# A fused attention and expert kernel: values of batches 0 and 1 in one transfer, 129-column rows, empty slots left out of the gathers, and a new order of steps

## The chip, the cores and the metric

The kernel runs on one core of a Trainium2 chip. The metric is the device time of one execution in microseconds. Three executions of the kernel before took 221.56, 222.04 and 222.4 us; the median is 222.04 us. A core has five engines with instruction streams of their own that meet only at semaphores: PE multiplies matrices, DVE and ACT work on tiles element by element, POOL issues nearly all DMA transfers here, and SP issues the first few. Each engine takes its instructions strictly in the order of its own stream.

## The reference

Attention without a softmax over pairs: queries are normalised over the head dimension, keys over the sequence, and per batch and head a 64x64 matrix is built from keys and values. The rows that come out are sorted by a hash of a token id to one of 8 experts, each two matrix products with a ReLU between.

```python
def _attn_ref(q, k, v):            # 8 batches, 8 heads, 576 rows, 64 columns
    q_s = np.exp(q - max);  q_s = q_s / (sum over columns + 1e-09)
    k_s = np.exp(k - max);  k_s = k_s / (sum over rows + 1e-09)
    kv = np.einsum('bhsd,bhse->bhde', k_s, v)
    return np.einsum('bhsd,bhde->bhse', q_s, kv)
def _moe_ref(x, token_ids, w1, w2):   # x: 4608 x 512, 8 experts, 512 -> 1024 -> 512
    expert_idx = token_ids * 2654435761 % 8
    for e in range(8):
        mask = expert_idx == e
        out[mask] = np.maximum(x[mask] @ w1[e], 0.0) @ w2[e]
```

## The kernel before

Each expert has 640 slots: 72 for each of the 8 batches, and 64 for rows beyond 72 of a batch (overflow). The prologue (`_Index.core`) finds on DVE and PE, from the token ids, which row of q belongs to which slot and leaves the row numbers in `gidx`; `row` holds the numbers of the output rows, with a number beyond the last row where a slot is empty. A gather (L396) fetches 128 rows of q for 128 slots by an indirect DMA, and a row number out of bounds is left out of it. In the kernel before only overflow gathers and the scatters of the results (L550) have such numbers; an empty slot of a main gather fetches some valid row.

After the prologue all work is cut into named steps, and the text `ORDER` is the order in which they are issued, on every engine at once: an engine's own stream is what is left of `ORDER` when the steps of other engines are struck out. `SWAP` names steps that go to the other one of DVE and ACT than is usual. `NAME*n` puts n idle matmuls of 512 columns (L346) into the step's PSUM bank ahead of it. The steps that the prediction speaks of:

- `G e_i`: gather of block i of expert e (`GO_i`: of overflow); `EQ`: its exponential on ACT (L406); `SM`: sums over columns and reciprocals on DVE (L416 to L418) for two or three blocks; `ML`: the scaling on DVE (L422); `TP`, `TC`: transposes on PE (L432) and their copy (L895).
- `K b`, `V b`: transfer of keys and values of batch b, values cast to f16. Batches 0 to 2 of the keys go through SP's queue, and values of 0 and 1 through POOL's, all issued before the ordered part. `EK b`: exponential of keys on ACT (L355, L356); `MK b`: ones in the last column of the values on ACT (L361), so that the product also gives the column sums; `KV b`: 20 matmuls of 129 columns (L373) into a bank of the PSUM tag "S"; `SC b`: reciprocal and scaling on DVE (L382 to L388) into `kvr`.
- `CNT`, `OVA`, `OHA`, `FND`, `FDD`, `QS`, `ROP`, `ROD`: the places of overflow rows, on DVE but for FND and ROP (PE). `ZO0`, `ZO1`: zeros for the overflow gathers, on DVE. `XP`, `XC`, `SH`, `SD`, `SI`, `SE`: the overflow rows' products (PE) and their evacuation.
- `ANY`: a register load of a flag and a branch on every engine (L835, L836) around a general path that is not taken with these ids. That path uses the PSUM banks of tag "S" on PE, DVE and ACT. At the end of the branch each engine sets a mark when all its earlier steps are done.
- `PP`, `PC`: products of queries with `kvr` (L443) and their evacuation into `XT` (L925), the input of the experts.
- `W e1_i`, `W e2_i`: fetches of an expert's weights, in halves or whole (`WHOLE`). Two buffers each, so a fetch for expert e waits for the last use by expert e-2; keys of batches borrow the buffers of expert 1 before.
- `A e_lo_i`: first layer (L523) with `R`, its ReLU; `B e_blk`: second layer (L545) with `C`, its evacuation; `S e_blk`: scatter.

DMA transfers of POOL's queue run one after the other; SP's queue runs beside it on the same 16 DMA engines.

Of the kernel before, what the change touches and what calls it, by code (L numbers as in the profile page):

```python
# [695 lines left out]
PC0_00 MLOb TP1_3 MK6 TC1_2 PP1_02 KV4 TC1_3 SD2 G3_1 PP1_03 PC1_02 TPO_3 EK7 SC5 MK7 SH0 SC4 TCO_3 G2_1 PC1_03 KV6
G2_2 TPO_2 SC6 TCO_2 PP0_41 SD3 KV7 SD0 PC0_41 PP0_43 PP0_42 SC7 XP2 PC0_42 PP0_40 PC0_43 PC0_40 PP1_01 XP3 PC1_01
PP0_61 XC2 G3_0 PP0_62 G3_2 PC0_61 PP1_43 XC3 PC0_62 W11_1 PP1_40 PC1_43 SI1 PC1_40 SI3 PP1_42 PP1_00 SE1 G3_3 PC1_42
PC1_00 A0_0_2 SI0 EQ3_1 SE3 PP0_63 A0_0_0 W11_0 PP0_60 G2_3 R0_0_2 SE0 W02_1 SI2 PC0_63 PP1_41 EQ3_0 R0_0_0 W02_0 G5_2
EQ2_1 G4_4 SM3a A0_0_1 R0_0_1 PC0_60 SE2 A0_0_3 PC1_41 ML3a R0_0_3 A0_576_0 EQ2_2 A0_432_0 A0_432_1 TP3_1 OV1 EQ2_0  # L700
R0_432_0 A1_0_0 R0_432_1 A1_320_3 G2_4 SM2a TP3_0 R1_0_0 ML2a TC3_1 EQ3_3 TC3_0 A1_0_3 TP2_1 R1_320_3 R1_0_3 TC2_1
W12_0 EQ3_2 A1_0_2 SM3b TP2_2 TC2_2 R0_576_0 TP2_0 A1_320_2 W12_1 EQ2_3 G6_2 G4_1 R1_320_2 ML3b B0_0 G5_3 TC2_0 B0_4
EQ2_4 C0_0 PP2_02 SM2b PC2_02 TP3_2 ML2b B0_1 TP3_3 A1_320_1 TC3_2 W21_0 G4_2 OV2 TP2_3 TC3_3 R1_0_2 TC2_3 TP2_4
A1_320_0 C0_4 C0_1 G7_2 G5_0 PP2_32 W21_1 R1_320_0 PC2_32 G4_3 TC2_4 B0_2 PP2_31 C0_2 PP2_03 PC2_31 PC2_03 A1_0_1
PP2_01 R1_0_1 B0_3 EQ5_3 S0_2 PP2_00 W31_0 OV4 PC2_00 R1_320_1 PC2_01 C0_3 B1_0 G5_1 PP2_33 G4_0 EQ5_2 EQ5_0 G7_3
# [10 lines left out]
R5_320_1 S1_0 TC6_4 R5_320_0 S2_2 OV6 W52_1 S1_3 A4_0_0 R4_0_0 TP6_0 S3_2 TP7_0 W52_0 C3_4 W61_0 A5_0_1 PP6_60 PC6_60
B4_1 A5_320_2 B4_4 TC7_0 C4_1 TC6_0 R5_0_1 S4_1 R5_320_2 C4_4 A5_0_0 R5_0_0 PP6_01 B4_0 C4_0 A5_0_2 R5_0_2 B4_3 PP6_00
PC6_01 PP6_31 PC6_00 PC6_31 B5_1 C4_3 S3_1 S3_4 C5_1 PP6_30 PP6_61 B4_2 PC6_30 C4_2 PC6_61 A6_0_2 A6_0_1 R6_0_1 B5_2
A6_320_1 R6_0_2 B5_3 W71_0 A6_0_0 S4_3 C5_3 B5_4 W62_0 OV7 R6_320_1 C5_4 A6_0_3 R6_0_0 R6_0_3 A6_320_0 C5_2 S4_2 B5_0
A7_0_2 S5_1 R6_320_0 A6_320_3 B6_0 R7_0_2 R6_320_3 S5_3 A6_320_2 S4_4 A7_320_0 C6_0 R6_320_2 S5_2 A7_320_2 R7_320_2  # L720
# [64 lines left out]

# [240 lines left out]
```

## Time and profile before

| | before |
|---|---|
| median of 3 runs | 222.04 us |
| profiled execution, its own time | 222.7 us |
| span of the profiled execution | 220.9 us |
| PE busy | 187.5 us (85%), 1534 matmuls |
| DVE busy | 133.6 us (60%) |
| ACT busy | 113.7 us (51%) |
| POOL busy | 120.2 us (54%) |
| DMA moved | 50.67 MB, 229 GB/s on average |

How to read it: the span runs from the first to the last instruction, and the execution's own time is 1.8 us longer, for what lies around it. Busy shares are averages over stages with different limits. The picture by slices of 5.5 us is this:

```profile
PE   3501098669899999999899999999999999999990
DVE  6989689989959796378583889530334312212230
DMA  6999999999999999999996969938999996751342
```

Each digit is the busy share of a slice in tenths. PE is at eight tenths or more from the tenth slice (49.7 us) to the end; DVE is at eight or more in all of the first eleven but the first and the fifth; the DMA engines are full from the second slice to the twenty-first (116 us).

### The profile page before, as it was taken

The page shows a single profiled execution, that of the slowest core. Times are in us where ns is not written, and L with a number is a line of the kernel's source. Part 1 is how long each engine was busy: PE and PEld are TensorE (multiplying, and loading weights), DVE is VectorE, ACT ScalarE, POOL GpSimd, SP SyncE. Part 2 cuts the span into 40 slices and gives each one's busy share as a digit, 9 for nine tenths or more (in the row PEclk, how much of TensorE's full clock was granted, in tenths as well). Part 3 has the DMA queues.
Part 4 walks back from the last instruction along what each step waited for, and adds up shares of the span by engine and source line. Part 5 has one row for each costly group of instructions (what it writes and reads, how often), then busy time and mean ns, then how long its engine had stood idle before and what let it go on. Part 6 is the DMA issues. An engine that isn't in the chain of part 4 may idle for free.

```text
span 220.9 us, 3984 instructions
## 1 busy us (share of the span) xinstructions
PE 187.5 (85%) x1534; PEld 122.2 (55%) x1534; DVE 133.6 (60%) x260; ACT 113.7 (51%) x183; POOL 120.2 (54%) x152
## 2 busy tenths in 40 slices
PE   3501098669899999999899999999999999999990
PEld 2501195437757756564576665657755655656550
DVE  6989689989959796378583889530334312212230
ACT  8142985899766763547475855215522333332201
POOL 7679766087267475577475028617551424171553
PEclk9999999999999999999999999999999999999998
DMA  6999999999999999999996969938999996751342
GB/s 203 327 329 287 330 391 384 240 314 305 240 326 254 271 251 309 227 234 206 261 223 164 205 144 158 213 104 153 277 237 237 207 167 225 136 179 47 136 175 98
DMA packets 12904, 50.67 MB, mean 229 GB/s; under 512 B 2522, under 2 KB 2522, under 8 KB 11344
## 3 DMA queue, kind: packets, MB, share of 16 engines
q0 software_dynamic: 12304, 46.66, 81.8%
q1 hardware_dynamic: 576, 3.71, 4.4%
q8 instruction: 13, 0.21, 0.4%
q14 instruction: 11, 0.09, 0.1%
HBM read 63.10 MB, written 10.49 MB: 333 GB/s over the span
## 4 chain that ended last, share of the span: by engine, by line
PE 51%; DVE 13%; issue 11%; POOL 6%; DMA 4%; POOLq 1%; ACT 1%; ACTq 0%
PE ph L523 24%; PE po L545 19%; POOL out_dram L550 6%; DMA w1r<-in_moe_w_dram 4%; DVE kvr L388 3%; PE t L432 3%; DVE rq L416 3%; DVE qs L422 2%; PE px L455 2%; PE t L443 1%; PE t L373 1%; PE t L472 1%; DVE XT L925 1%; DVE rec L384 1%; DVE XTov L478 1%
## 5 line engine op out<-in xcount | busy, mean ns | idle before, releaser
L523 PE MATMUL ph<-XT,w1r 128*128 128x320 f16 (+2 forms) x512 | 75.3, 297 | 1.3 <-DMA w1r<-in_moe_w_dram 1.3
L545 PE MATMUL po<-w2r,hT 128*128 128x512 f16 (+2 forms) x328 | 74.5, 374 | 0.0
L536 ACT ACTIVATE hT<-ph 128x640 f16<-128x640 f32 (+3 forms) x59 | 41.6, 709 | 57.6 <-PE ph L523 50.7
L550 POOL DMA_INDIRECT out_dram<-ob,sidx x40 | 41.6, 1041 | 51.7 <-DVE ob L956 32.5
L523 PEld LDWEIGHTS <-w1r 128*128 128x128 f16 x544 | 49.1, 98 | 23.0 <-DMA w1r<-in_moe_w_dram 1.6
L396 POOL DMA_INDIRECT raw<-in_q_dram,gidx x36 | 44.0, 1223 | 19.9 <-issue 6.9
L545 PEld LDWEIGHTS <-hT 128*128 128x128 f16 x328 | 31.2, 98 | 31.0
L956 DVE TENSOR_SCALAR ob<-po 128x512 f32<-128x512 f32 x32 | 21.6, 682 | 43.3 <-PE po L545 35.7
L416 DVE TENSOR_REDUCE rq<-qs 128x16 f32<-128x1024 f16 (+1 forms) x18 | 23.9, 1329 | 3.9 <-ACT qs L406 3.8
L406 ACT ACTIVATE qs<-raw 128x512 f16<-128x512 f32 x36 | 21.8, 630 | 7.3 <-DMA raw<-in_q_dram,gidx 5.5
L422 DVE TENSOR_TENSOR qs<-qs,rq 128x1024 f16<-128x1024 f16 (+1 forms) x18 | 24.0, 1337 | 0.2
L895 DVE COPY qT<-t 128x512 f16<-128x512 f16 (+1 forms) x19 | 9.9, 528 | 13.5 <-PE t L432 12.8
L432 PE MATMUL t<-ident,qs 128*128 128x128 f16 x160 | 13.7, 222 | 2.2 <-DVE qs L422 1.7
L432 PEld LDWEIGHTS <-qs 128*128 128x128 f16 x160 | 11.1, 100 | 4.5 <-ACT qT L895 1.8
L508 POOL DMA_DIRECT2D w1r<-in_moe_w_dram x14 | 8.2, 586 | 9.2 <-PE ph L523 6.7
L373 PE MATMUL t<-v,w1r 128*128 128x129 f16 x64 | 7.0, 266 | 5.3 <-ACTq L836 5.3
L508 POOL DMA_DIRECT2D w2r<-in_moe_w_dram x14 | 8.3, 595 | 5.5 <-PE po L545 3.0
L954 ACT ACTIVATE ob<-po 128x512 f32<-128x512 f32 (+2 forms) x9 | 4.9, 552 | 11.7 <-PE po L545 11.6
L925 ACT CAST XT<-t 128x288 f16<-128x288 f32 (+2 forms) x17 | 6.5, 400 | 7.8 <-PE t L443 7.7
L925 DVE CAST XT<-t 128x288 f16<-128x288 f32 (+2 forms) x15 | 6.5, 447 | 5.2 <-PE t L443 5.1
L931 ACT CAST XT<-px 128x864 f16<-128x864 f32 (+1 forms) x7 | 5.7, 810 | 6.7 <-PE px L455 6.7
L256 PE MATMUL po<-Z,AO 128*128 128x8 f16 x18 | 0.6, 175 | 9.9 <-DVE AO L244 9.9
(128 smaller groups left out, 197.5 us busy)
## 6 DMA issues: line engine op xcount, KB each, us to landing
...
```

The costliest lines, as they stand in the source:

```text
L396: nc.gpsimd.indirect_dma_start(out=raw[:, :], out_offset=None, in_=self.q[:, :], in_offset=bass.IndirectOffsetOnAxis(ap=idx[:, i:i + 1], a ...
L406: self.nc.scalar.activation(q16[:, i].rearrange("p h d -> p (h d)"), raws[i][:, :], ACT.Exp)
L416: nc.vector.reduce_sum(rv, qv, axis=AX.X)
L422: nc.vector.tensor_tensor(out=qf, in0=qf, in1=rv.rearrange("p i h -> p (i h)").unsqueeze(2) .to_broadcast([128, (hi - lo) * H_, DH_]), op= ...
L432: nc.tensor.transpose(pv[:, r, 128 * j:128 * j + 128], rq16[1][:, i + j, 2 * r:2 * r + 2, :] .rearrange("p h d -> p (h d)"), self.ident[:])
L508: self.nc.gpsimd.dma_start(w[what - 1][:, f], src[e, :, f])
L523: nc.tensor.matmul(p, lhsT=w1r[:, dc, f[i] * 128:(f[i] + 1) * 128], rhs=X[:, dc, :], start=(dc == 0), stop=(dc == DC - 1))
L536: self.nc.scalar.activation(to, fro, ACT.Relu)
L545: nc.tensor.matmul(po[:, 0:d.stop - d.start], lhsT=hT[:, fc, blk * 128:(blk + 1) * 128], rhs=w2r[:, fc, d], start=(fc == 0), stop=(fc == F ...
L550: sc = self.nc.gpsimd.indirect_dma_start(out=self.out[:, :], out_offset=bass.IndirectOffsetOnAxis(ap=self.ix.sidx[:, e, blk:blk + 1], axis=0),
L925: (A if other(f"PC{e}_{lo}{r}", r % 2 == 0) else V)(X[:, es, r, lo * CELL:hi * CELL], px[e, r, lo])
L956: nc.vector.tensor_scalar(out=obs[e, blk][:, d], in0=po[e, blk, x][:, 0:d.stop - d.start], scalar1=1.0 / SX, scalar2=None, op0=ALU.mult)
```

## The change

- Rows of values have 129 columns instead of 130, in memory and on the chip (a row starts at an odd multiple of 2 bytes every second time). One tile holds the values of a pair of batches. The pair (0, 1) comes in one transfer and gets its ones in one step, `MK0`; the other pairs still come in two.
- `gidx` has a number beyond the last row where a slot is empty, so that every gather leaves empty slots out: two more DVE instructions in the prologue, and three instead of one ahead of the first use of `gidx`. The ten buffers of the gathers are set to zero first, by ten ACT copies of 128x512 f32 from one column.
- The weights of the first layer of expert 7 come in halves.
- `ORDER` and `SWAP` are new for the whole kernel. `ANY` stands after `SM0a` and `QS`, `KV1` has six idle matmuls, `KV2` none.

```diff
-VW = 130
+VW = 129
@@ core
-        V.tensor_tensor(out=gidx[:].rearrange("p e k -> p k e"), in0=ppv,
-                        in1=base[:].unsqueeze(2).to_broadcast([128, BPE, E_MOE]), op=ALU.add)
         V.tensor_scalar(out=row[:], in0=ppv, scalar1=0.0, scalar2=2.0 * N_TOK, op0=ALU.is_equal, op1=ALU.mult)
-        V.tensor_tensor(out=row[:], in0=row[:], in1=gidx[:].rearrange("p e k -> p k e"), op=ALU.add)
-        V.tensor_scalar(out=gidx[64:128, 0:E_MOE:2, BPE - 1], in0=tail[64:128, 1:E_MOE:2],
-                        scalar1=float(S_ * (B_ - 1) - 1), scalar2=None, op0=ALU.add)
+        V.tensor_tensor(out=row[:], in0=row[:], in1=base[:].unsqueeze(2).to_broadcast([128, BPE, E_MOE]), op=ALU.add)
+        V.tensor_tensor(out=gidx[:].rearrange("p e k -> p k e"), in0=row[:], in1=ppv, op=ALU.add)
+        V.tensor_scalar(out=none[u], in0=tail[u, 1:E_MOE:2], scalar1=0.0, scalar2=2.0 * N_TOK, op0=ALU.is_equal,
+                        op1=ALU.mult)
+        V.scalar_tensor_tensor(out=gidx[u, 0:E_MOE:2, BPE - 1], in0=tail[u, 1:E_MOE:2],
+                               scalar=float(S_ * (B_ - 1) - 1), in1=none[u], op0=ALU.add, op1=ALU.add)
+        V.tensor_tensor(out=row[:], in0=row[:], in1=ppv, op=ALU.add)
@@ clear
+        for _ in range(NRAW):
+            nc.scalar.copy(self.raw()[:], zero[:].to_broadcast([128, D_MOE]))
@@ kernel
+            def vpart(b):
+                return slice(0, C9) if b - b % 2 in PAIRS else slice(b % 2 * C5, C5 + b % 2 * (C5 - 1))
             def load_v(b):
-                v16s[b] = apool.tile([128, (C5 - b % 2) * NPAIR, VW], F16, tag=f"v16_{b % 2}", name=f"v16_{b}", bufs=2)
-                nc.gpsimd.dma_start(v16s[b][:].rearrange("p c d -> p (c d)"),
-                                    part(v, b, NPAIR * VW))
+                if b % 2 == 0:
+                    v16s[b // 2] = apool.tile([128, C9 * NPAIR, VW], F16, tag="v16", name=f"v16_{b // 2}", bufs=2)
+                f = vpart(b)
+                f = slice(f.start * NPAIR, f.stop * NPAIR)
+                nc.gpsimd.dma_start(v16s[b // 2][:, f].rearrange("p c d -> p (c d)"),
+                                    v[b // 2, :, f.start * VW:f.stop * VW])
@@ order
-WHOLE = ((6, 1), (6, 2), (7, 1), (7, 2),)
+WHOLE = ((6, 1), (6, 2), (7, 2),)
+PAIRS = (0,)
-ZO0 CNT MK0 OVA G0_2 OHA FND G0_1 G0_0 EK1 V2 ZO1 MK1 EQ0_0 G0_3 EK0 EQ0_2 EQ0_1 K3 EK2 FDD ANY V3 KV1 G0_4 SM0a G1_1
-ML0a TP0_1 EQ0_3 EK3 KV0 GO_0 SC1 EQ0_4 EQ1_1 MK2 MK3 TC0_1 QS GO_1 SM0b K4 TP0_0 ROP G1_2 TC0_0 TP0_2 EQO_0 EQO_1
-G1_0 SC0 K5 ML0b SMOa KV2*9 EQ1_0 GO_2 ROD GO_3 KV3 MLOa TC0_2 TP0_3 EQ1_2 TC0_3 EQO_2 TPO_0 TCO_0 G1_3 V4 SC3 SC2
...
+G0_0 CNT OVA OHA EK0 ZO1 G0_2 EK1 EQ0_2 G0_1 EK2 V2 EQ0_1 FND EQ0_0 G1_2 MK0 ZO0 MK2 K3 G0_4 FDD SM0a G0_3 QS
+ANY KV1*6 EQ0_4 KV0 G1_3 GO_0 ML0a GO_1 TP0_0 K4 SC0 EQ0_3 KV2 EK3 EQ1_2 V3 TP0_1 SM0b TC0_0 ROP ML0b EQO_0
+TP0_3 EQO_1 G1_0 SC2 TC0_3 TP0_2 GO_3 TC0_1 G1_1 MK3 KV3 SMOa TC0_2 EK4 MLOa K5 TPO_1 SC3 TPO_0 TCO_0 EQ1_3
+EQ1_1 K6 SC1 TCO_1 XP1 EQ1_0 EQO_3 PP0_00 XC1 EK5 V4 SM1a XP0 PP0_03*4 XC0 PC0_03 PC0_00 PP0_02 SH2 PC0_02
+SM1b TP0_4 TC0_4 MK4 GO_2 EQO_2 V5 ML1b ML1a V6 ROD TP1_1*4 MK5 TP1_0 TC1_1 EK6 K7 SH1 TP1_3 SMOb TC1_0 SD1
+SD2 KV5 MK6 TP1_2 KV4 TC1_2 V7 W01_1 PP1_02 TC1_3 W01_0 MLOb SH0 G3_1 G2_2 G2_1 G2_3 PC1_02 TPO_2 G3_0 SH3
+TCO_2 SC5 PP0_01 G6_4 PP1_03 SD3 PC0_01 SC4 EK7 PC1_03 KV6 G2_4 TPO_3 PP0_42 PC0_42 PP1_01 TCO_3 G2_0 MK7 KV7
+SD0 PP1_00 PC1_01 XP2 SC6 PC1_00 W11_0 PP0_40 PC0_40 PP0_41 XC2 PP0_43 PC0_43 SC7 PC0_41 XP3 PP0_63 PC0_63
+PP1_40 W11_1 G3_2 PP1_43 XC3 PC1_43 SI2 SI3 SE2 PP0_60 PC1_40 PP0_61 W02_1 EQ2_2 A0_0_0 EQ3_1 PC0_61 W02_0 SI0
...
+W12_0 SE1 OV1 A0_0_1 PP1_42 PC1_41 ML3a A0_432_0 G5_1 A0_576_0 SM2a PC1_42 R0_432_0 TP3_0 TP3_1 A0_432_1
+R0_0_1 EQ2_3 ML2a A1_320_0 G4_2 OV3 G7_2 R0_432_1 A1_320_2 R1_320_0 G5_3 A1_0_3 R1_320_2 TC3_1 TP2_1 EQ2_4
...
+SM3b TP2_0 TC2_0 G4_3 A1_320_1 W12_1 TP2_3 EQ4_0 C0_2 TC2_3 G5_0 PP2_01 R1_320_1 ML3b B0_0 PP2_00 PC2_01
...
```

## Rows read from the trace of the kernel before

**Rows 1.** Stages: start:end, length, PE, PEld, DVE, ACT, POOL busy (instructions), clock, DMA, GB/s.

```profile
22.00:27.00 5.00, 0.00 (x0) 0.10 (x1) 3.09 (x11) 4.97 (x6) 3.80 (x5) 1.00 1.04 344
27.00:44.00 17.00, 14.65 (x168) 11.53 (x167) 15.51 (x37) 13.23 (x21) 8.21 (x10) 1.00 1.04 333
44.00:62.30 18.30, 14.78 (x201) 11.39 (x200) 16.64 (x39) 15.89 (x29) 10.51 (x11) 1.00 1.04 297
62.30:216.00 153.70, 152.31 (x1095) 94.31 (x1091) 79.58 (x124) 69.63 (x114) 79.60 (x85) 1.00 0.83 202
```

**Rows 2.** Chain of waits in order of time: start, length in us, what.

```profile
27.06 2.34 PE t L373 x20
```

**Rows 3.** The branch's line L836: duration in ns, first and last start in us.

```profile
L836 DVEq EVENT_SEMAPHORE  x1: 21/21/21, 23.9 to 23.9; - x1
L836 ACTq EVENT_SEMAPHORE  x1: 17/17/17, 27.0 to 27.0; - x1
```

**Rows 4.** The line L373 of the KV steps, same columns.

```profile
L373 PEldq EVENT_SEMAPHORE  x4: 51/51/51, 23.9 to 56.8; - x4
```

**Rows 5.** Timeline of ACT: start, length, what, and in brackets the idle time before.

```profile
2.13 4.25 ACT L336 COPY kvr<-zero 128x512 f16<-128x512 f16 x8
13.36 0.23 ACT L361 COPY v<-two 128x40 f16<-128x40 f16 x1 [6.99 <-DMA v<-in_v_dram]
13.49 1.91 ACT L355 ACTIVATE w1r<-kraw 128x2048 f16<-128x2048 f32 x1
18.20 0.22 ACT L361 COPY v<-two 128x32 f16<-128x32 f16 x1 [2.15 <-DMA v<-in_v_dram]
20.66 0.63 ACT L406 ACTIVATE qs<-raw 128x512 f16<-128x512 f32 x1 [2.24 <-DMA raw<-in_q_dram,gidx]
21.20 1.89 ACT L355 ACTIVATE w1r<-kraw 128x2048 f16<-128x2048 f32 x1
23.52 1.13 ACT L406 ACTIVATE qs<-raw 128x512 f16<-128x512 f32 x2
```

**Rows 6.** Timeline of DVE.

```profile
11.56 0.23 DVE L164 TENSOR_TENSOR row<-row,gidx 128x40 f32<-128x40 f32 x1
24.68 1.75 DVE L416 TENSOR_REDUCE rq<-qs 128x24 f32<-128x1536 f16 x1 [1.74 <-ACT qs L406]
27.02 1.76 DVE L422 TENSOR_TENSOR qs<-qs,rq 128x1536 f16<-128x1536 f16 x1
29.43 0.16 DVE L382 TENSOR_SCALAR rec<-t 128x4 f32<-128x4 f32 x1 [0.65 <-PE t L373]
30.70 1.14 DVE L280 TENSOR_SCALAR Q<-rowi,ov 128x512 f16<-128x512 f16 x4
33.51 0.16 DVE L382 TENSOR_SCALAR rec<-t 128x4 f32<-128x4 f32 x1
57.67 0.69 DVE L478 CAST XTov<-t 128x512 f16<-128x512 f32 x1
58.95 0.86 DVE L388 TENSOR_TENSOR kvr<-t,rec 64x256 f16<-64x256 f32 x2
```

**Rows 7.** Timeline of PE.

```profile
33.14 2.17 PE L346 MATMUL t<-rowi,ident 128*128 128x512 f16 x9
36.01 0.22 PE L373 MATMUL t<-v,kt 128*128 128x129 f16 x1
36.30 0.22 PE L373 MATMUL t<-v,kt 128*128 128x129 f16 x1
62.33 1.63 PE L523 MATMUL ph<-XT,w1r 128*128 128x432 f16 x8
105.70 2.08 PE L523 MATMUL ph<-XT,w1r 128*128 128x320 f16 x14 [1.26 <-DMA w1r<-in_moe_w_dram]
```

**Rows 8.** Timeline of POOL.

```profile
62.41 1.02 POOL L396 DMA_INDIRECT raw<-in_q_dram,gidx  x1 [1.32 <-DMA w1r<-in_moe_w_dram]
```

**Rows 9.** The page's part 3: the DMA queue that POOL fills; packets, MB, share.

```profile
q0 software_dynamic: 12304, 46.66, 81.8%
```

More of the change, by code (lines that the diff above doesn't have):

```diff
@@ L42 @@
 MAINC = B_ * CELL
+NRAW = 10
 PLACE = [4 * (b // 4) + 2 * (b % 2) + b % 4 // 2 for b in range(B_)]
@@ L357, in expk, with mark @@
         return k16.rearrange("p (c f) -> p c f", c=C5 - 1), k16t
-    def mark(self, b, v16):
-        n = (C5 - b % 2) * NPAIR
-        self.nc.scalar.copy(v16[:, 0:n, 128:VW], self.two[:].unsqueeze(1).to_broadcast([128, n, VW - 128]))
+    def mark(self, v16):
+        n = v16.shape[1]
+        self.nc.scalar.copy(v16[:, :, 128:VW], self.two[:].unsqueeze(1).to_broadcast([128, n, VW - 128]))
     def keys(self, b, k16s, v16s):
@@ L373, in keys @@
                 nc.tensor.matmul(pkv[:, r // 2, r % 2, 0:129], lhsT=k16t[:, f] if last else k16[:, c, f],
-                                 rhs=v16s[e][:, c * NPAIR + r, 0:129] if last else v16s[b][:, c * NPAIR + r, 0:129],
+                                 rhs=v16[:, (c if last else b % 2 * C5 + c) * NPAIR + r, 0:129],
                                  start=(c == 0), stop=last)
@@ L394, in gather @@
         for i in range(lo, hi):
-            raw = into[i] if into else self.qpool.tile([128, D_MOE], F32, tag="qraw", bufs=10)
+            raw = into[i] if into else self.raw()
             nc.gpsimd.indirect_dma_start(
@@ L681 @@
 CUTS = [((0, 432), (432, MAINC), (MAINC, CAP))] + [((0, HN), (HN, CAP))] * (E_MOE - 1)
-WHOLE = ((6, 1), (6, 2), (7, 1), (7, 2),)
+WHOLE = ((6, 1), (6, 2), (7, 2),)
+PAIRS = (0,)
 SWAP = set("""
-TC1_0 SD1 PC0_00 SD2 TCO_3 PC0_43 PC0_62 R0_0_3 TC2_0 C0_0 C0_2 R1_320_1 PC2_01 C0_3 PC2_30 PC2_63 PC2_61
-R2_320_1 C2_4 PC4_31 C2_0 C4_2 C6_4 R7_0_0 C7_4a C7_4b
+TCO_0 PC0_03 TC1_0 TC1_2 PC0_42 TCO_3 SD0 PC1_01 PC0_43 R1_320_2 TC3_1 TC2_1 TC2_0 PC2_01 PC2_00 R1_0_2 TC3_3
+C1_0 C1_4 PC2_03 R3_0_2 R3_320_1 PC4_01 PC4_31 R5_0_1 C4_0 R5_320_3 R7_320_3 C7_4a C7_4b
@@ L696 @@
[L696 to L705, printed above, removed]
@@ L716 @@
[L716 to L720, printed above, removed]
@@ new lines @@
+R5_320_3 B5_3 C5_3 A5_0_0 S4_4 TC6_4 TP7_2 TC7_2 PC6_00 S2_3 R5_0_0 A5_0_3 R5_0_3 B4_2 PP6_60 PP6_30 C4_2
+W61_0 B5_4 W71_1 PC6_60 PC6_30 PP6_31 W71_0 B5_0 PP6_01 C5_4 PC6_31 PC6_01 S1_4 PP6_61 B4_1 PC6_61 S5_3 A6_0_1
+C5_0 A6_320_2 R6_0_1 B5_1 R6_320_2 A6_320_1 S5_4 A6_0_3 C5_1 R6_320_1 A6_0_0 R6_0_3 R6_0_0 A7_0_0 A6_320_0
+B5_2 R6_320_0 A6_0_2 R7_0_0 W62_0 R6_0_2 C5_2 S5_0 C4_1 A7_0_3 A7_0_2 R7_0_2 B6_0 W72_0 A6_320_3 C6_0 R6_320_3
+R7_0_3 S4_2 B6_1 A7_0_1 B6_3 C6_1 A7_320_1 B6_4 C6_3 S4_0 S6_0 R7_0_1 R7_320_1 A7_320_3 S4_3 B6_2 A7_320_2
@@ L784, in load_k, with mark @@
                 (nc.gpsimd if b > 2 else nc.sync).dma_start(kraws[b][:], part(k, b, D_MOE))
+            def vpart(b):
+                return slice(0, C9) if b - b % 2 in PAIRS else slice(b % 2 * C5, C5 + b % 2 * (C5 - 1))
             def load_v(b):
-                v16s[b] = apool.tile([128, (C5 - b % 2) * NPAIR, VW], F16, tag=f"v16_{b % 2}", name=f"v16_{b}", bufs=2)
-                nc.gpsimd.dma_start(v16s[b][:].rearrange("p c d -> p (c d)"),
-                                    part(v, b, NPAIR * VW))
+                if b % 2 == 0:
[4 more added lines that the diff above has]
+                                    v[b // 2, :, f.start * VW:f.stop * VW])
+            def mark(b):
+                f = vpart(b)
+                at.mark(v16s[b // 2][:, f.start * NPAIR:f.stop * NPAIR])
             at = _Attention(nc, tc, q, k, v, cpool, qpool, apool, ps)
@@ L796 @@
                 load_k(b)
-            for b in range(2):
-                load_v(b)
+            for b in (0, 1):
+                if b == 0 or 0 not in PAIRS:
+                    load_v(b)
             load_k(2)
@@ L848 @@
             for b in range(B_):
-                if b > 1:
+                if b > 1 and (b % 2 == 0 or b - 1 not in PAIRS):
                     add(f"V{b}", load_v, b)
@@ L853 @@
                 add(f"EK{b}", expk, b)
-                add(f"MK{b}", lambda b: at.mark(b, v16s[b]), b)
+                if b % 2 == 0 or b - 1 not in PAIRS:
+                    add(f"MK{b}", mark, b)
                 add(f"KV{b}", lambda b: pkvs.update({b: at.keys(b, k16s, v16s)}), b)
```

39 lines of the change are left out of this document (23 added, 16 removed).

## The prediction

> **What bounds the kernel now.** I read the stages first, then the chain of waits, then the timelines of the engines around the first products. From 62.3 us on PE is busy 152.31 of 153.70 us [rows 1]; the only long stop there is 1.26 us at 105.70, for weights of an expert [rows 7]. What happens before 62.3 us therefore sets the end, and the reader is to see there that PE is not the bound: it does nothing from 22 to 27 us and is idle 2.35 us of the next 17.0 and 3.52 us of the 18.3 after that [rows 1]. DVE is: it works 15.51 of 17.0 and 16.64 of 18.3 us [rows 1], without a stop between the reciprocal of batch 0 (SC0, 33.51) and the end of the scaling of the last batch (SC7, 58.95 + 0.86 = 59.81) [rows 6]. The first layer of expert 0 starts at 62.33 [rows 7], 2.52 us after SC7. The DMA engines are full until then too, at 1.04 [rows 1], and the weights for that start land just before it: POOL's next gather waited 1.32 us for them, until 62.41 [rows 8]. So two limits lie within a microsecond at 62.3: DVE's chain and the weights.
>
> DVE's chain began late because of the branch. PE's first product, KV1, starts at 27.06 [rows 2]. Before it PE's sequencer took a wait at 23.9, as DVE set its mark at 23.9 [rows 3, 4], and its first matmul went right after ACT's mark at 27.0 [rows 3]. I read this as KV1 waiting for the marks of both, since its bank is one that the general path uses.
>
> **The marks in the new order.** DVE's steps ahead of the branch were ZO0, CNT, OVA, OHA, ZO1, FDD; now SM0a and QS stand ahead of it too. ACT's were MK0, EK1, MK1, EQ0_0, EK0, EQ0_2, EQ0_1, EK2; now they are EK0, EK1, EQ0_2, EK2, EQ0_1, EQ0_0, MK0, MK2.
>
> ACT first. Eight copies of 128x512 took 4.25 us from 2.13 [rows 5], 0.53 each; ten more of that size end at 2.13 + 18 x 0.53 = 11.7. Their output is f32 instead of f16; the nearest f32 form, EQ, is 1.13 us for two [rows 5], 0.57 each, so 12.1 is the other end. ACT sat idle from 6.4 to 13.36 before [rows 5], which hides them. Keys of batches 0 and 1 had landed when EK1 ran at 13.49 [rows 5]; EK0 can start between 11.7 and 13.5, say 12.6. One EK is 23.52 - 21.20 = 2.32 us [rows 5], so EK1 is done at 17.2. EQ0_2 needs the second gather. The values of batch 1 landed at 18.20 and the third gather after them at 20.66 [rows 5], 0.82 us for each, so the second lands at 19.8. The joint transfer of values changes nothing in that: its bytes are those of the two, less 1/130, and the gathers queue behind all of it as before. EQ0_2 19.8 to 20.4, EK2 to 22.7, two EQ at 1.13 us to 23.85, two MK at 0.22 each to 24.3: ACT's mark comes at 24.3 instead of 27.0.
>
> DVE next. Two more instructions in the prologue of about 0.2 us (nearest row 0.23) cost 0.4 us [rows 6] and ZO0's move gives 1 us back to CNT, but FDD then waits behind both ZO steps; all of this is hidden, since SM0a waited 1.74 us for ACT already [rows 6]. SM0a starts with EQ0_0's end at 23.85 instead of 24.68, takes 27.02 - 24.68 = 2.34, QS 1.14 [rows 6]: DVE's mark comes at 27.3, now the later of the two. PE starts at about 27.4, 0.3 us later than before, although its operands wait from 24.3.
>
> **Six idle matmuls, then KV1, then KV0.** PE works at its slower level after the pause: the granted clock is given as 1.00 throughout [rows 1], but 20 matmuls of KV1 take 2.34 us [rows 2], and five at 36 us take 36.30 - 36.01 = 0.29 [rows 7], 1.16 for 20; that is 1.2 against 2.4 GHz. Nine idle matmuls at the upper level took 2.17 us [rows 7], 0.24 each with their last one's drain, 0.22 without; at the lower one I take twice that, 6 x 0.44 = 2.6 us. The Trainium skill (TensorE: Matmul & The Clock Gate, Part 1) gives 426.7 ns between starts at the lower level, 2.56 us for six, and by it the sum below is the same to 0.05 us. The rise came between 29.4 and 33.1 us, with PE at work since 27.06 [rows 2, 7]. KV0 so ends between 31.1 (all at the upper level: 27.4 + 1.4 + 2 x 1.16) and 34.7 (all at the lower: 27.4 + 2.6 + 2 x 2.34). I take 33.4: idle matmuls and KV1 at the lower level to 32.3, KV0 at the upper.
>
> What waits for it: ML0a ends at 27.3 + 1.76 = 29.1 [rows 6], and the next on DVE is SC0, which needs KV0. DVE stands still from 29.1 to 33.5, with SM0b, ML0b and the rest queued behind. Before it had 0.65 us of that sort, as SC1 came first and KV1 without idle matmuls [rows 6].
>
> **From there to the end.** SC0 starts at 33.5, as it did before, but with SC1 (30.70 - 29.43 = 1.27) and SM0b (33.51 - 30.70 - 1.14 = 1.67) [rows 6] still to do. Up to SC7 the new order takes from DVE one cast of 0.69 (two of SD became one) [rows 6], and moves two casts out (PC0_03, PC0_00) against two copies of about the same size in (TCO_0, TC1_2); net -0.7, and between 0 and -1.4 if the swaps cost unlike. SC7 ends at 33.5 + 26.3 + 1.27 + 1.67 - 0.7 = 62.0, 2.2 us later than before, and the first layer starts at 64.5. Its weights are there by then: the same transfers stand ahead of them, so they land by 62.4 or sooner.
>
> After that start PE has as much to do as before (columns counted matmul by matmul, the two orders differ by 0.1 us). The stop of 1.26 us goes: expert 3's first use comes 2.2 us later by the clock and 2.9 us later in PE's own order. For new stops I put 0.4 us, between 0 and the old 1.26. The ten spare idle matmuls (14 against 24) lay where PE waited for DVE and give nothing. The tail is the same chain of B7, C7 and S7.
>
> Costed at nothing, with their cover: the halves of expert 7's first layer (the queue has air late, 0.83 over the stage [rows 1]); MK with one column (0.22 before [rows 5]); V4's wait for KV1 as well as KV0 (the full queue ahead of it). Rows of 258 bytes: no row shows a matmul on such a start. Between nothing (the same 129 columns) and a halved rate, 8 x 1.16 = 9.3 us of PE time, of which some 5.9 us fit into its idle time up to 62.3; I take nothing, the nearest rows [rows 7]. Skipped rows: the token ids leave 216 of the 4608 main slots empty, 0.44 MB of 46.66 [rows 9], but only 66 of them (0.14 MB, with the narrower values 0.17 MB) before the first weights: 0.6 us at 297 GB/s [rows 1], off the path while DVE is the later one.
>
> Sum: +2.2 - 1.26 + 0.4 = +1.3 us. The profiled execution took 222.7 us around its span of 220.9; I put the difference on the median, 222.04: 223.3 us, its own range 221.8 to 225.0 by the ends of KV0 (-2.3, +1.3, the former stopped by the weights) and of the new stops.
>
> **Rivals.** (1) KV1 waits for ACT's mark alone. For it: the matmul itself went with ACT's mark [rows 3]; against it: the sequencer's wait that ended with DVE's [rows 4]. Then PE starts at 24.3 and KV0 is done near 30.3, SC7 ends near 59, and the weights set the start: 62.3 - 0.5 = 61.8. That is -0.5, and -1.26 for the stop: 220.2 us, faster. If the chip still fetches the empty rows, it is 220.7.
> (2) The marks hold as I say, but the early rise of the clock and DVE's lighter list give most of it back: KV0 at 32, SC7 at 60.6, start at 63.1, +0.8 - 1.26 + 0.4: 222.0 us, no change. For it: the time of the rise is known only to 4 us.
> (3) Fetches come late in the new order. W12_1 stands behind seven gathers of 0.82 us each, and W61 whole behind the scatter S4_4. Each stop of the kind seen at 105.70 may cost 1 to 3 us; with two of them 225.8 us. Against it: by count of PE's work the first use still lies 9 us or more behind each issue.
>
> **How the numbers follow.** Chances: forecast 0.47, (1) 0.22, (2) 0.19, (3) 0.12. What a measurement can tell from no change is 0.5%, 1.1 us. Slower: 0.31 of the forecast's, all of (3), 0.02 of (2): 0.45. Within: 0.15, 0.15 of (2), 0.03 of (1): 0.33. Faster: the rest of (1) and a little of the others, 0.22. The range must reach to both sides: 219.8 to 226.0.
>
> **What would show it.** In the new profile: DVE's mark near 27.3, after ACT's near 24.3; PE's first idle matmul right after it; DVE idle some 4 us ahead of L382 near 33.5; the last L388 near 62 and the first L523 near 64.5; no stop for w1r near 105; bytes of the queue down by 0.4 MB. It is wrong if idle matmuls start by 25 us, if DVE's pause is under 2 us, or if L523 starts before 62.5.

## The result and the profile after

The changed kernel takes 224.13 us (median of six runs, 223.32 to 224.7) against 222.03 us (six runs, 221.56 to 222.4): ratio 1.0095, 95% interval 1.0075 to 1.0115. It is about 2 us slower. The profiled execution took 224.47 us around a span of 222.6 us; before it was 222.7 around 220.9.

The stages of the changed kernel, columns as in [rows 1], with its own border at 65.4 us:

```profile
22.00:27.00 5.00, 0.00 (x0) 0.00 (x0) 4.27 (x15) 2.27 (x6) 4.08 (x6) 1.00 1.00 384
27.00:44.00 17.00, 12.90 (x142) 10.34 (x142) 11.47 (x24) 11.30 (x17) 8.73 (x10) 0.90 1.01 337
44.00:65.40 21.40, 16.34 (x214) 12.21 (x215) 19.12 (x48) 18.38 (x34) 11.86 (x12) 1.00 1.03 270
65.40:216.00 150.60, 150.60 (x1082) 93.49 (x1080) 81.39 (x128) 66.72 (x108) 76.72 (x85) 1.00 0.82 198
```

The last stage is now full: PE works all of its 150.60 us. The loss lies ahead of it. DVE worked 15.51 of the 17 us from 27 us on [rows 1]; now it is 11.47. The marks of the branch, whose line is now L861 (duration in ns, first and last start in us):

```profile
L861 ACTq EVENT_SEMAPHORE  x1: 17/17/17, 25.1 to 25.1; - x1
L861 DVEq EVENT_SEMAPHORE  x1: 21/21/21, 27.3 to 27.3; - x1
```

ACT's mark came 1.9 us earlier than before and DVE's 3.4 us later [rows 3]. PE's timeline from there (the KV steps are L383 now, the idle matmuls L356, the first layer L533):

```profile
27.51 2.72 PE L356 MATMUL t<-rowi,ident 128*128 128x512 f16 x6 [6.58 <-DVEq L861]
30.02 0.64 PE L383 MATMUL t<-v,w1r 128*128 128x129 f16 x4
...
32.73 0.53 PE L383 MATMUL t<-v,w1r 128*128 128x129 f16 x4
33.10 0.22 PE L383 MATMUL t<-v,kt 128*128 128x129 f16 x1
...
65.42 1.63 PE L533 MATMUL ph<-XT,w1r 128*128 128x432 f16 x8
```

The first row names its releaser: DVE's mark. Four matmuls of KV1 take 0.64 us, the slower of the two levels; in the group at 32.73, in the middle of KV0, the upper one sets in. DVE over the same time, and the end of its scaling:

```profile
27.46 1.76 DVE L432 TENSOR_TENSOR qs<-qs,rq 128x1536 f16<-128x1536 f16 x1 [0.15 <-DVEq L861]
33.92 0.16 DVE L392 TENSOR_SCALAR rec<-t 128x4 f32<-128x4 f32 x1 [4.70 <-PE t L383]
...
61.97 0.16 DVE L392 TENSOR_SCALAR rec<-t 128x4 f32<-128x4 f32 x1 [0.24 <-PE t L383]
62.17 0.18 DVE L394 RECIPROCAL rec<-rec 128x4 f32<-128x4 f32 x1
62.38 0.86 DVE L398 TENSOR_TENSOR kvr<-t,rec 64x256 f16<-64x256 f32 x2
```

ML0a (L432) ends at 29.22, and then DVE stands for 4.70 us until KV0 is done. SC7 ends at 63.24 (before 59.81 [rows 6]), the first L533 starts 2.18 us later, at 65.42 instead of 62.33 [rows 7]: 3.09 us late. From that start to PE's last matmul it is 152.10 us (to 217.52), against 153.54 (62.33 to 215.87): 1.44 us come back, and the stop of 1.26 us [rows 7] isn't there. The span grew by 3.09 - 1.44 + 0.05 (the tail) = 1.7 us.

### The profile page after: what moved, and what is told of

Read it like the earlier page. It is cut to its first block, busy times and chain, and to the rows that moved or that the text cites. A ratio compares the mean times of both kernels' runs of the same rounds, so it can differ in the third digit from the quotient of the medians.

```text
span 222.6 us, 3962 instructions
## 1 busy us (share of the span) xinstructions
PE 187.1 (84%) x1524; PEld 121.8 (55%) x1524; DVE 135.6 (61%) x264; ACT 117.2 (53%) x190; POOL 118.5 (53%) x152
## 3 DMA queue, kind: packets, MB, share of 16 engines
q0 software_dynamic: 12304, 46.19, 80.3%
## 4 chain that ended last, share of the span: by engine, by line
PE 53%; issue 15%; DVE 9%; POOL 7%; ACT 2%; POOLq 1%; DVEq 0%
PE ph L533 23%; PE po L555 19%; POOL out_dram L560 6%; PE t L442 3%; PE t L383 3%; DVE rq L426 3%; DVE qs L432 2%; DVE kvr L398 2%; PE t L453 1%; PE t L356 1%; PE px L465 1%; PE t L482 1%; ACT w2r L365 1%; POOLq L1047 1%; DVE rq L428 0%
## 5 line engine op out<-in xcount | busy, mean ns | idle before, releaser
L533 PE MATMUL ph<-XT,w1r 128*128 128x320 f16 (+2 forms) x512 | 74.7, 297 | 0.0
L546 ACT ACTIVATE hT<-ph 128x640 f16<-128x640 f32 (+3 forms) x56 | 39.3, 712 | 61.2 <-PE ph L533 61.2
L533 PEld LDWEIGHTS <-w1r 128*128 128x128 f16 x544 | 49.3, 98 | 21.4
L982 DVE TENSOR_SCALAR ob<-po 128x512 f32<-128x512 f32 x36 | 24.2, 681 | 48.6 <-PE po L555 48.6
L406 POOL DMA_INDIRECT raw<-in_q_dram,gidx x36 | 42.4, 1177 | 18.8 <-issue 7.0
L432 DVE TENSOR_TENSOR qs<-qs,rq 128x1024 f16<-128x1024 f16 (+1 forms) x18 | 23.8, 1330 | 0.4 <-DVEq L861 0.2
L453 PE MATMUL t<-qT,kvr 128*128 128x72 f16 (+1 forms) x96 | 8.6, 206 | 3.9 <-ACT XT L951 1.9
L921 DVE COPY qT<-t 128x512 f16<-128x512 f16 (+1 forms) x17 | 9.1, 541 | 3.9 <-PE t L442 3.8
L951 ACT CAST XT<-t 128x288 f16<-128x288 f32 (+2 forms) x19 | 7.4, 407 | 7.0 <-PE t L453 6.8
L453 PEld LDWEIGHTS <-kvr 128*128 128x128 f16 x96 | 6.4, 98 | 7.5 <-issue 3.6
L548 DVE TENSOR_SCALAR hT<-ph 128x640 f16<-128x640 f32 x7 | 5.7, 821 | 7.6 <-PE ph L533 7.6
L356 PE MATMUL t<-rowi,ident 128*128 128x512 f16 x14 | 4.8, 484 | 6.6 <-DVEq L861 6.6
L921 ACT COPY qT<-t 128x512 f16<-128x512 f16 x11 | 6.3, 587 | 6.5 <-PE t L442 6.5
```

The source lines that it names most:

```text
L406: nc.gpsimd.indirect_dma_start(out=raw[:, :], out_offset=None, in_=self.q[:, :], in_offset=bass.IndirectOffsetOnAxis(ap=idx[:, i:i + 1], a ...
L432: nc.vector.tensor_tensor(out=qf, in0=qf, in1=rv.rearrange("p i h -> p (i h)").unsqueeze(2) .to_broadcast([128, (hi - lo) * H_, DH_]), op= ...
L453: nc.tensor.matmul(pv[:, :, i * CELL:(i + 1) * CELL], lhsT=self.kvrs[b][:, r, :], rhs=qT[:, r, q0 + es.start:q0 + es.stop, b * CELL:(b + 1 ...
L533: nc.tensor.matmul(p, lhsT=w1r[:, dc, f[i] * 128:(f[i] + 1) * 128], rhs=X[:, dc, :], start=(dc == 0), stop=(dc == DC - 1))
L546: self.nc.scalar.activation(to, fro, ACT.Relu)
L982: nc.vector.tensor_scalar(out=obs[e, blk][:, d], in0=po[e, blk, x][:, 0:d.stop - d.start], scalar1=1.0 / SX, scalar2=None, op0=ALU.mult)
```

## The experiments

The first four were run together, against 222.14 us for the kernel before (29 runs). Two theories stood: the late start is paid by the order (DVE's mark behind SM0a and QS, six idle matmuls ahead of KV1), or by something else that is new (data, DVE's list).

**Idle matmuls out.** Of the changed kernel, one word of the order:

```diff
-ANY KV1*6 EQ0_4 KV0
+ANY KV1 EQ0_4 KV0
```

> The changed kernel without the six idle matmuls ahead of KV1. Theory (the idle matmuls lie on the path: DVE's mark, idle matmuls, KV1, KV0, SC0): KV1 starts at 27.5, both products run at the lower level, 2 x 2.34, KV0 ends at 32.2 instead of 33.9, DVE's pause shrinks from 4.70 to 3.0, first L523 at 63.7 instead of 65.42; time 222.4. Rival (the idle matmuls pay for themselves, since KV0 comes out at the upper level after them): KV0 ends at 33.9 as now, time 224.1.

Measured 222.71 us (222.43 to 223.53), ratio to before 1.0026 (1.0010 to 1.0042). That is 1.4 us below the changed kernel: the idle matmuls are on the path. DVE and PE in it (the last row is a stop in the second layer):

```profile
31.73 0.16 DVE L392 TENSOR_SCALAR rec<-t 128x4 f32<-128x4 f32 x1 [2.64 <-PE t L383]
```

```profile
63.22 1.63 PE L533 MATMUL ph<-XT,w1r 128*128 128x432 f16 x8
...
91.36 2.75 PE L555 MATMUL po<-w2r,hT 128*128 128x512 f16 x12 [0.51 <-DMA w2r<-in_moe_w_dram]
```

SC0 starts 2.19 us and the first L533 2.20 us earlier than in the changed kernel. Part of that is given back at 91.36, where PE waits 0.51 us for weights; the changed kernel has no such stop.

**The branch earlier.** The mark ahead of SM0a and QS, idle matmuls kept:

```diff
-FDD SM0a G0_3 QS
-ANY KV1*6
+FDD ANY SM0a G0_3 QS
+KV1*6
```

> The changed kernel with the branch ANY right after FDD, ahead of SM0a and QS; the six idle matmuls stay. Theory (PE is held by the later of the marks of DVE and ACT): DVE's mark at 23.8, ACT's at 24.3, PE starts at 24.4 instead of 27.5, KV0 ends at 30.8, DVE's pause before SC0 is 1.6 instead of 4.70, SC7 at 60.1; then the weights set the first L523 at 62.0 to 62.4; time 221.0. Rival 1 (KV1 waits for ACT alone, or for its operands): PE starts at 27.5 again, time 224.1. Rival 2 (DVE's chain alone sets the first L523): it starts at 62.3 whatever the weights do, the time is the same 221.0; e3 tells it.

Measured 222.85 us (221.85 to 224.09), ratio 1.0026 (1.0005 to 1.0046): the direction as expected, 1.3 us instead of 3. PE starts 2.44 us earlier, with ACT's mark now, since DVE's comes before it:

```profile
25.07 2.72 PE L356 MATMUL t<-rowi,ident 128*128 128x512 f16 x6 [4.22 <-ACTq L859]
```

That settles that PE waits for both marks: with ACT's at 25.1 in both kernels, PE's start followed DVE's mark where that came later. SC0 starts at 31.11, 2.81 us earlier, but the first L533 only 1.96 us, at 63.46. Part of the gain is lost in between: DVE waits 0.59 us for PE ahead of TC1_2, at 52.74, which it doesn't in the changed kernel.

**Both together.**

```diff
-FDD SM0a G0_3 QS
-ANY KV1*6
+FDD ANY SM0a G0_3 QS
+KV1
```

> The changed kernel with both edits: branch after FDD, no idle matmuls. Theory (behind DVE's chain the landing of expert 0's weights is the next limit): KV0 ends at 29.1, no pause of DVE, SC7 near 58.5, but the first L523 stays at 62.0 to 62.4; time 220.7 to 221.1, within 0.4 us of the run with the early branch alone. Rival (no such limit): first L523 at 60.7, time 219.4.

Measured 222.83 us (221.59 to 224.76), ratio 1.0026 (1.0001 to 1.0052), no better than either, and above the 220.7 to 221.1 us of the theory. SC0 now starts at 29.65, 4.27 us earlier than in the changed kernel, and the first L533 only 2.70 us earlier. What is late now? The last scaling of SC7 on DVE, POOL's queue and PE at the end of the stage:

```profile
59.67 0.86 DVE L398 TENSOR_TENSOR kvr<-t,rec 64x256 f16<-64x256 f32 x2
```

```profile
62.84 1.00 POOL L406 DMA_INDIRECT raw<-in_q_dram,gidx  x1 [0.86 <-DMA w1r<-in_moe_w_dram]
```

```profile
62.72 1.63 PE L533 MATMUL ph<-XT,w1r 128*128 128x432 f16 x8
```

SC7 ends at 60.53, and the first layer starts 2.19 us later, as in the changed kernel (2.18), without a wait for weights: DVE's chain still sets that start, and not the weights, as the theory had it. They are close behind, though: POOL's row stands 0.26 us behind their landing in the chain of waits, so they landed at 62.58, 0.14 us ahead of the first layer. The gain was lost on DVE, which takes 30.88 us from SC0 to SC7 instead of 29.32. Its longest new wait is the one ahead of TC1_2. ACT, PE and DVE on the way to it:

```profile
49.46 0.26 ACT L371 COPY v<-two 128x16 f16<-128x16 f16 x1 [1.28 <-DMA v<-in_v_dram]
```

```profile
50.20 0.38 PE L442 MATMUL t<-ident,qs 128*128 128x128 f16 x4 [1.67 <-ACT qT L919]
```

```profile
51.98 0.42 DVE L919 COPY qT<-t 128x512 f16<-128x512 f16 x1 [1.00 <-PE t L442]
```

ACT waits 1.28 us for the values of batch 5 to land (MK5); its next step, TC1_1, is late by that, PE's TP1_3 waits for TC1_1, and KV5 and TP1_2, which DVE's TC1_2 waits for, stand behind TP1_3 in PE's stream. In the changed kernel MK5 runs at 51.42 without a wait. So the next limit of the new order is a transfer too, but of values, 13 us ahead of the first weights. No run was made that changes this transfer alone.

**Six idle matmuls in the kernel before.** The other way round, one edit on the kernel before:

```diff
-FDD ANY V3 KV1 G0_4
+FDD ANY V3 KV1*6 G0_4
```

> The kernel before with six idle matmuls ahead of KV1 as its one edit. Theory (what holds KV1 back holds DVE's whole chain back): KV1 ends 2.6 us later, at 32.0, DVE waits 3.2 instead of 0.65 us for it, the first L523 comes at 64.5 to 64.9, the stop of 1.26 us at 105.70 goes; time 223.0 to 223.6. Rival (DVE catches up, since KV0 then runs at the upper level): 222.0.

Measured 224.25 us (223.81 to 224.63), ratio 1.0088 (1.0063 to 1.0113): this alone costs as much as the whole change. DVE and PE of it:

```profile
31.79 0.16 DVE L382 TENSOR_SCALAR rec<-t 128x4 f32<-128x4 f32 x1 [2.75 <-PE t L373]
```

```profile
64.79 1.44 PE L523 MATMUL ph<-XT,w1r 128*128 128x432 f16 x7
...
107.09 2.08 PE L523 MATMUL ph<-XT,w1r 128*128 128x320 f16 x14 [0.27 <-DMA w1r<-in_moe_w_dram]
```

DVE's wait of 0.65 us ahead of SC1 [rows 6] became 2.75, the first layer starts 2.46 us late, and the stop of 1.26 us shrinks to 0.27: PE comes to it 2.38 us later (106.82 against 104.44), and the weights only 1.39 us later (107.09 against 105.70). The loss is partly given back by the stop, as in the changed kernel.

**The data alone.** Three more kernels, with 222.21 us for the kernel before (23 runs). The first is the changed kernel with the orders of before (MK0 where MK1 stood, W71 whole):

```diff
-ORDER, SWAP, WHOLE of the changed kernel
+ORDER (MK1 -> MK0, old MK0 out), SWAP, WHOLE of the kernel before
```

> The changed kernel with the orders of the kernel before (ORDER, SWAP and the whole W71 of before; MK0 stands where MK1 stood, since the pair has one step). What is left of the change is its data: the pair in one transfer, 129 columns, skipped empty slots, zeroed buffers, the longer prologue. Theory (only the order costs): the first L523 near 62.5 us in the trace, 221.4 to 222.2 us; the stop of 1.26 us at 105.70 us shorter than before if the missing 0.4 MB matter to it. Rival (the data part costs): 223.5 us or more, with the loss ahead of the first L523.

Measured 222.36 us (221.68 to 223.31), ratio 1.0013 (0.9996 to 1.0029): no difference that can be told. First L533 at 62.42. The pair in one transfer, 129 columns, ten zeroed buffers, the longer prologue and the skipped rows together cost at most some 0.6 us by the interval; the order costs the rest. In the profiled execution the stop at 105.7 us was absent; the two kernels below in the same old order say how far that goes.

**Empty slots fetched again in the changed kernel.** The prologue of before in the changed kernel:

```diff
-V.tensor_tensor(out=row[:], in0=row[:], in1=base[:]...)
-V.tensor_tensor(out=gidx[:]..., in0=row[:], in1=ppv, op=ALU.add)
+V.tensor_tensor(out=gidx[:]..., in0=ppv, in1=base[:]..., op=ALU.add)
...
+V.tensor_tensor(out=row[:], in0=row[:], in1=gidx[:]..., op=ALU.add)
```

> The changed kernel with the prologue's row numbers of before: empty slots fetch a valid row again (q0 back up by about 0.44 MB). Theory (the new order took away the stop of 1.26 us that the kernel before had in its second stage): as the changed kernel, 223.9 to 224.4 us, PE without a stop after its first L523. Rival (the missing bytes took it away): a stop of 0.7 to 1.3 us after the first L523 comes back, 224.8 to 225.4 us.

Measured 223.87 us (222.85 to 224.11), ratio 1.0078 (1.0056 to 1.0101): as the changed kernel, with no stop after the first layer's start. The queue's row of the page:

```profile
q0 software_dynamic: 12304, 46.63, 81.7%
```

In the changed kernel that row has 46.19 MB, so an empty slot's row is really not moved (0.44 MB); it buys nothing here. This profiled execution (222.85 us, the lowest of its runs) shows more by accident. In it the clock rose sooner (KV is L379, the reciprocal step L388, the first layer L529 here):

```profile
27.23 2.72 PE L352 MATMUL t<-rowi,ident 128*128 128x512 f16 x6 [6.59 <-DVEq L857]
29.74 0.61 PE L379 MATMUL t<-v,w1r 128*128 128x129 f16 x4
...
30.25 0.39 PE L379 MATMUL t<-v,w1r 128*128 128x129 f16 x4
...
63.92 1.63 PE L529 MATMUL ph<-XT,w1r 128*128 128x432 f16 x8
```

```profile
32.43 0.16 DVE L388 TENSOR_SCALAR rec<-t 128x4 f32<-128x4 f32 x1 [3.50 <-PE t L379]
```

Groups of four take 0.39 us from 30.25 on, where the changed kernel's execution had 0.64 until 32.73. SC0 starts 1.49 us earlier than there, the first L529 1.50 us earlier, PE ends 1.50 us earlier (216.02). PE's start is 0.28 us of that (27.23 instead of 27.51), the sooner rise 1.2 us. In the same order of steps, with a few other instructions in the prologue, the 1.5 us of KV0's end are 1.5 us of the end.

**Empty slots skipped in the kernel before.** The reverse of that edit, with the ten zeroed buffers:

```diff
+V.tensor_tensor(out=gidx[:]..., in0=row[:], in1=ppv, op=ALU.add)
...
+        for _ in range(NRAW):
+            nc.scalar.copy(self.raw()[:], zero[:].to_broadcast([128, D_MOE]))
```

> The kernel before with one part of the change: row numbers out of bounds for empty slots, the longer prologue, the ten zeroed buffers. Theory (the order took the stop away): the stop near 105.7 us stays, 222.0 to 222.5 us. Rival (the missing bytes took it away): the stop is under 0.3 us and the time 220.8 to 221.4 us, below both kernels.

Measured 222.34 us (221.3 to 223.77), ratio 1.0004 (0.9983 to 1.0025). The stop stays:

```profile
105.85 2.08 PE L533 MATMUL ph<-XT,w1r 128*128 128x320 f16 x14 [1.06 <-DMA w1r<-in_moe_w_dram]
```

So the missing bytes alone don't take it away. In the new order it is gone, at a later start of PE and also at 62.72 (both edits together). Why it was absent in the one execution of the old order above, with the first layer at 62.42, isn't settled.

**PE warmed ahead of the branch.** If the lower level is what makes KV1 and KV0 long, idle matmuls where PE idles anyway should be worth more than idle matmuls behind the wait. A new step puts 18 of them into a bank that isn't waited for; those on KV1 go (kernel before in these two runs: 221.85 us, 20 runs):

```diff
-K3 G0_4 FDD SM0a G0_3 QS
-ANY KV1*6
+K3 G0_4 FDD HOT*18 SM0a G0_3 QS
+ANY KV1
...
+            add("HOT", at.bank, "T")
```

> The changed kernel without the six idle matmuls on KV1, and with 18 idle matmuls put on PE ahead of the branch (behind FDD in the order), into a PSUM bank of the tag T that nothing waits for; they fill PE's idle time from about 21 to 27.5 us and end before the mark that KV1 waits for. Theory (what costs is that PE comes to KV1 and KV0 at the lower level, with or without idle matmuls): KV1 starts at about 27.5 us as before but at the upper level, 1.3 us, KV0 ends at about 30.2 us instead of 33.88, SC0 starts some 3.5 us earlier than in the changed kernel, and the first L533 then waits for its weights and not for DVE, at 62.0 to 62.8 us: 221.2 to 222.0 us, at or below the kernel before. Rival 1 (the level is not up at KV1 in spite of the idle matmuls): as the changed kernel without its idle matmuls, 222.4 to 223.0 us. Rival 2 (DVE's chain has other waits that come up): SC0 early but the first L533 not before 63.5 us, 222.5 us or more.

Measured 222.74 us (221.66 to 224.63), ratio 1.0047 (1.0021 to 1.0074). PE, DVE and POOL in it:

```profile
27.86 0.39 PE L383 MATMUL t<-v,w1r 128*128 128x129 f16 x4 [1.07 <-DMA raw<-in_q_dram,gidx]
...
63.20 1.64 PE L533 MATMUL ph<-XT,w1r 128*128 128x432 f16 x8
```

```profile
30.33 0.16 DVE L392 TENSOR_SCALAR rec<-t 128x4 f32<-128x4 f32 x1 [1.17 <-PE t L383]
```

```profile
63.41 1.00 POOL L406 DMA_INDIRECT raw<-in_q_dram,gidx  x1 [1.51 <-DMA w1r<-in_moe_w_dram]
```

KV1 and KV0 run at the upper level (0.39 us for four), SC0 starts 3.59 us earlier than in the changed kernel. That much is the theory's. The time is not. SC7 ends at 60.76, only 2.48 us earlier: DVE waits 0.86 us ahead of TC1_2, since ACT waits 1.40 us for the values of batch 5 (MK5 at 49.66). The first layer then starts 2.44 us behind SC7 instead of 2.18; these 0.26 us are a wait for its weights, which come at 63.15 us, later than the 62.33 at which the kernel before starts that layer. So most of what is lost is lost as in rival 2, in DVE's other waits, though less than it said.

**The same in the old order.** On the kernel with the data part alone:

```diff
-EQ0_1 K3 EK2 FDD ANY V3 KV1
+EQ0_1 K3 EK2 FDD HOT*18 ANY V3 KV1
```

> The data part of the change with the orders of the kernel before (as the earlier run of that), and the same 18 idle matmuls on PE ahead of the branch. Theory (the front is bound by DVE and by the transfers there, since KV1 and KV0 at the lower level lie beside DVE's scaling): KV1 takes 1.3 us instead of 2.33, SC1 starts at most 0.6 us earlier, the first L533 at 62.0 to 62.4 us, 221.6 to 222.3 us. Rival (the level of the clock holds the front here as well): the first L533 under 61.5 us, 220.8 us or less.

Measured 223.31 us (222.54 to 223.69), ratio 1.0055 (1.0037 to 1.0072): slower than both expectations. PE's branch shows why (duration in ns, first and last start in us):

```profile
L859 PEldq COMPARE_BRANCH  x1: 6106/6106/6106, 22.5 to 22.5; - x1
L859 PEldq EVENT_SEMAPHORE  x1: 51/51/51, 28.6 to 28.6; - x1
```

PE's sequencer stayed in the branch for 6.1 us, past the end of the idle matmuls ahead of it at 27.55 (0.40 us without them), and its event is at 28.6. KV1 starts at 29.01 instead of 26.95, later than with a PE at the lower level. I had counted the idle matmuls as hidden; they hold PE in its own branch, and KV1 stands behind that in PE's stream. In the kernel above the same row is 5.9 us, but DVE's mark was late there anyway, so that KV1 lost only 0.35 us. The stop for weights is back in this run too (0.91 us at 106.45).

**PE kept busy in its later pauses.** In the changed kernel the granted clock falls near 40 us (third number from the end):

```profile
39.00:40.00 1.00, 0.38 (x4) 0.26 (x4) 0.95 (x3) 1.00 (x4) 0.00 (x0) 0.92 1.01 428
40.00:41.00 1.00, 0.96 (x10) 0.96 (x10) 0.93 (x3) 1.00 (x2) 0.00 (x0) 0.50 0.92 393
```

The trace before had no such rows. The last pair adds idle matmuls in the pauses behind the branch, once to the warmed kernel, once to the changed one (kernel before: 222.3 us, 17 runs):

```diff
-KV2 ... TP0_3 ... TP0_2 ... KV3 ... TPO_1 ... XP1
+KV2*4 ... TP0_3*3 ... TP0_2*2 ... KV3*2 ... TPO_1*3 ... XP1*4
```

> The kernel of the run with 18 idle matmuls ahead of the branch, with more idle matmuls in the pauses of PE behind it (4 ahead of KV2, 3 of TP0_3, 2 of TP0_2, 2 of KV3, 3 of TPO_1, 4 of XP1), so that PE isn't sparsely used between 30 and 42 us. Theory (the level falls to 1.2 GHz between 36 and 47 us in traces of the new order, in some executions longer than in others, and the slow products there hold DVE now and then; that is the part of the loss that the profiled runs don't show): no fall in the trace, 221.9 to 222.4 us and a narrower spread than the 221.66 to 224.63 us without them. Rival (the fall lies beside DVE's work and costs nothing, the weights' landing sets the first L533): 222.5 to 223.0 us with or without it.

Measured 223.04 us (221.85 to 224.34), ratio 1.0037 (1.0015 to 1.0058), above the theory and at the rival's upper end. The spread, 2.5 us against 3.0, is no difference that 12 runs of each can tell.

> The changed kernel, idle matmuls on KV1 included, with the same idle matmuls in PE's pauses between 34 and 45 us (4 ahead of KV2, 3 of TP0_3, 2 of TP0_2, 2 of KV3, 3 of TPO_1, 4 of XP1). Theory (the fall of the level near 40 us costs): 223.0 to 223.6 us, no rows at the lower level behind 34 us. Rival (it costs nothing, DVE's chain from SC0 on has no wait for PE there): 223.8 to 224.4 us, as the changed kernel.

Measured 226.98 us (225.8 to 228.89), ratio 1.0226 (1.0190 to 1.0261), against every expectation. The level did stay up, 1.00 in the stage:

```profile
27.00:44.00 17.00, 13.73 (x160) 9.43 (x160) 12.08 (x26) 11.01 (x16) 8.41 (x10) 1.00 1.02 349
```

From SC0 to SM1a DVE took 11.90 us (33.37 to 45.27) against 11.61 with the fall (33.92 to 45.53). In the changed kernel DVE has one wait in that stretch, of 0.10 us. So the fall cost DVE nothing there, and that theory is dropped. The added time came mostly behind it: the first L533 starts at 67.36, and DVE alone has one wait of 1.65 us more:

```profile
56.43 0.42 DVE L919 COPY qT<-t 128x512 f16<-128x512 f16 x1 [1.65 <-PE t L383]
```

The products it reads were done at 54.62; what held it isn't settled.

## Why the prediction was right

It said 223.3 us, 1.3 above the kernel before; measured was 224.13, 2.1 above. The range, 219.8 to 226.0, was wide enough for every rival, so what counts is the mechanism, and it is the one that ran. By its steps:

- **The marks.** Forecast ACT 24.3, DVE 27.3, PE at 27.4; in the trace ACT's steps end at 24.34 (its mark at 25.1), DVE's mark is at 27.3 and PE starts at 27.51. Rival 1, ACT's mark alone, fell with that row, and with the run that put the branch earlier.
- **Idle matmuls, KV1, KV0.** Forecast 32.3 and 33.4; measured 32.39 and 33.88. The six took 2.51 us start to start (27.51 to 30.02), 0.42 each, against 0.44 assumed. KV0's first part was still at the lower level; that is 0.5 us. The Trainium skill (TensorE: Matmul & The Clock Gate, Part 1) gives 426.7 ns from start to start at the lower level, and the 0.42 us of this trace agree.
- **DVE's pause.** Forecast some 4 us ahead of SC0; measured 4.70.
- **From SC0 to SC7.** This is the term that was mis-sized: forecast 28.5 us (33.5 to 62.0), measured 29.32. The list of DVE's casts is shorter by the 0.7 I counted, but I took that list to run without new waits. I had also read DVE before as without a stop between the two; it has one of 0.47 us:

```profile
47.61 0.42 DVE L895 COPY qT<-t 128x512 f16<-128x512 f16 x1 [0.47 <-PE t L432]
```

  The chain of waits in the changed kernel (start, length, what) leaves DVE for ACT ahead of SC7:

```profile
57.84 1.81 ACT w2r L365
59.68 0.63 ACT kt L366
60.33 0.27 ACT v L371
60.60 0.04 issue
60.64 1.31 PE t L383 x20
61.97 0.16 DVE rec L392
```

  EK7, MK7 and KV7 hold SC7 for 0.24 us, and DVE waits 0.32 us ahead of PC0_42 and 0.10 us ahead of MLOa, 0.66 us in three places against 0.47 in one (TC1_0) before. The other 0.6 us is in longer steps, counted from start to start without waits: five SM take 8.56 us, where four of before (6.57) and the 1.67 that I added make 8.24; five ML take 6.04 instead of 5.84; SC and the casts add 0.04 each. With KV0's 0.5 us, and 2.18 us from SC7 to the first layer where I put 2.5, the start is late by 3.09 us and not by 2.2.
- **After the start.** Forecast -1.26 for the stop and +0.4 for new ones; measured -1.44, with no stop for weights at all. The run of idle matmuls in the kernel before shows one reason why it goes: PE's later start gained 0.99 us on the weights. The new order has a share of its own, since the stop is absent with both edits too, at a start of 62.72. The +0.4 was for nothing here; in four repairs of the new order (below) a new stop of 0.18 to 0.51 us does come, near 91 us. Rival 3 had no stop to show in the profiled execution.
- **The sum.** +3.09 - 1.44 + 0.05 against +2.2 - 0.86. The errors, 0.9 too little before that start and 0.6 too little given back behind it, have opposite signs; that they leave only 0.4 us in the trace is luck.
- **Costed at nothing.** The data part in the old order: ratio 1.0013 (0.9996 to 1.0029). 20 matmuls on the new rows took 1.30 us at the upper level, as 20 of the old did (KV3 of before, 36.64 to 37.94): no cost of the odd starts. The ten zero copies ended at 11.56, forecast 11.7.
- **Rival 2** (the early rise gives it back) is what the execution with the clock back at 30 us comes near to: KV0 ends at 32.40, the first layer starts at 63.92. It names a spread from execution to execution more than another case.

One thing the forecast had only as a remark: DVE's chain and the weights lie within a microsecond. Four repairs of the new order (no idle matmuls, branch earlier, both, PE warmed) bring SC0 2.2 to 4.3 us earlier, and all end between 222.71 and 222.85 us, with the first layer at 63.22, 63.46, 62.72 and 63.20. It starts 2.18 or 2.19 us behind SC7 in the first three, as in the changed kernel, and 2.44 in the last; only there do the weights hold it, for 0.26 us. They land 0.71, 0.29, 0.14 and 0.05 us ahead of it. So DVE's chain stayed the first limit, with the weights next to it, and the rest of the gain went into DVE's new wait ahead of TC1_2 (none, 0.59, 1.00 and 0.86 us) and into the stop near 91 us (0.51, 0.36, 0.18 and 0.44 us). The row of POOL behind the weights is at 62.77, 63.43, 62.84 and 63.41 in the four, and at 62.41 and 62.01 in two kernels of the old order. Why the weights land later in the new order isn't settled; the DMA engines moved 295 to 303 GB/s from 27 to 62 us in those four kernels and 313 in the kernel before. With both edits the profiled execution (222.09 us) is 0.7 us below the median of its runs (222.83), so its trace shows one of the better executions. No version was faster than the kernel before.
